# Where VectorE's first instructions of an expert's run stand in its queue: free, or behind the last instructions of the run before

## The chip, the cores and the metric

The kernel runs on one core of one Trainium2 chip. The metric is the device time of one execution in microseconds (us). Five engines work side by side, each through a queue of its own, in order: TensorE (PE in the profile; PEld are its weight loads), VectorE (DVE), ScalarE (ACT), GpSimd (POOL) and SyncE (SP), which issues most of the DMAs.

## The reference

Two blocks follow each other. A gated linear recurrence makes 3072 tokens of 384 numbers; then a router picks one of eight experts for each token, and the token goes through that expert's two layers.

```python
for t in range(S):
    state = alpha[:, :, t, :, None] * state + einsum(k[:, :, t], v[:, :, t])
    y[:, :, t] = einsum(q[:, :, t], state)
...
logits = xn @ en.T / tau                 # xn, en: rows of length 1
expert_idx = argmax(logits, axis=1)
gate_w = softmax(logits) at expert_idx
for e in range(E):
    h = maximum(x[mask] @ w1[e], 0.0)    # 384 -> 1024
    out[mask] = gate_w[mask, None] * (h @ w2[e])
```

## The kernel before, in words

The first part (to about 160 us) is the recurrence, in 24 chunks of 128 tokens. Each token's row, with its logits, is written to a scratch area in DRAM, sorted by expert. The second part takes the experts one after another: run `i` is the `i`-th expert in turn, `run(i)` at L1255. Run 0 has one block of 128 tokens left (two were done early), each of the runs 1 to 7 has three blocks, and behind each run a conditional part (`run_extra`, L1319) does half a block of 64 more tokens if the expert has that many. The branch of that part reads the count on every engine (L1322, L1326).

What a run of three blocks (`pair` in the code) does:

- `first_layer_blocks` (L1080): the first layer in 20 products of sums of quarters, in place of 24 plain ones. A product (L1095) is two matmuls in the code and four in the trace. The products go through four PSUM banks, called A, G, D and B. `put` (L1103, ScalarE) copies a bank into the hidden tile `hT`; `add` (L1109, VectorE) adds a bank to it. A bank is used again and again within the run, so the next product into D can start only when the `add` that reads D is done.
- `mix_hidden` (L1016, VectorE) makes sums of hidden quarters in `hT_m`; `mix_weights` (L1005) makes four sums of quarters of `w2` in `w_m`. `mix_weights` is on GpSimd, except in run 1, where it is on VectorE (L1266). `second_layer` (L967) does one block plainly, and `second_layer_pair` (L1179) two blocks with these sums; its three `gated` steps (L1202) on VectorE read the banks and make the output rows `y`, which `scatter` (L860, GpSimd) sends out by indirect DMA.
- For the next expert: `prepare` (L940) turns its tokens over on TensorE; `begin_gates` (L944) is the first part of its gates, five small VectorE instructions on 128x4 or 128x32 elements (`gtop`, `xg` times `used`, `none`, `sx`, `gsh`) that need only that its rows `xg` have arrived from DRAM; `gates_norm` and `gates_end` are the rest. `mix_first_weights` (L1041, GpSimd) makes 16 sums of quarters of `w1`, `mix_first_rows` (L1054, VectorE) 13 sums of the tokens, for the products of the next run.

Run 0 is not of that kind: it goes through `first_layer` (L957), `prepare_gates(1)` (L950), `mix_first_rows(1)` and one `second_layer`, whose scaling by the gate (L976) is on VectorE.

What sets the order: the program is traced in the order of the text. A planner at compile time then lays out each engine's queue. An instruction whose inputs are there can be placed ahead of earlier ones that still wait, also ahead of the branch of a conditional part, which is placed as one unit. `tc.issue_after(x)` puts what is traced under it behind `x` in `x`'s queue; it orders the queue and waits for nothing. The kernel uses this for chains by hand. `by_dve` (L988) puts every call behind the one before it and keeps the latest in the list `dve`; `by_act` (L993) does so on ScalarE with `act`, `product` on TensorE with `pe`. In a pair run everything that VectorE does up to `gates_end` is in that chain, in this order: in run 1 the four `mix_weights` first, then `begin_gates(i + 1)`, then the 14 `add`s. At the head of a run the list is set anew:

```python
dve[:] = [] if pair else ready
```

An empty list means that the first call of the chain has no place to keep. So a run's first VectorE calls may be placed far ahead, in the middle of the run before.

Of the kernel before, what the change touches and what calls it, by code (L numbers as in the profile page):

```python
# [27 lines left out]
def kernel(  # L28
# [12 lines left out]
    nc = tc.nc  # L41
# [113 lines left out]
    def blocks_run(i):  # L155

        return NC - EARLY if i == 0 else NC

    def slots(i):
        return [(t, P) for t in range(blocks_run(i))] + [(blocks_run(i), HALF)]  # L160
# [40 lines left out]
    with ExitStack() as c1:  # L201
# [517 lines left out]
        for s in range(NS + 3):  # L719
# [64 lines left out]
            if 4 <= s < 4 + NXG * (NC + 1):  # L784
                i, t = divmod(s - 4, NC + 1)
# [41 lines left out]
    with ExitStack() as c3:  # L827
# [66 lines left out]
        def gates(xg, gate, col, n, has=None):  # L894
            known = gates_logits(xg, col, n, has)
            for t in range(n):
                gates_square(xg, known, t)
            gates_norm(known, n)
            return gates_end(gate, known, n)
# [21 lines left out]
        def gates_square(xg, known, t, by=freely):  # L921
            x2 = yp.tile([P, DM], FP32, name="gx2", bufs=1)
            by(nc.scalar.activation, x2, xg[:, t, 0:DM], AF.Square, accum_out=known[1][:, t])

        def gates_norm(known, n, by=freely, by_act=freely):
            sh, sq = known
            shp = [P, n, E]
            by_act(nc.scalar.activation, sq, sq, AF.Sqrt)
            by(nc.vector.tensor_scalar, sq, sq, 1e-6, None, ALU.add)
            by(nc.vector.reciprocal, sq, sq)  # L930
            by(nc.vector.tensor_tensor, sh, sh, sq.to_broadcast(shp), ALU.mult)
            by_act(nc.scalar.activation, sh, sh, AF.Exp)

        def gates_end(gate, known, n, by=freely):
            sh, _ = known
            by(nc.vector.tensor_reduce, gate.unsqueeze(2), sh, axis=AX.X, op=ALU.add)
            by(nc.vector.tensor_scalar, gate, gate, 1e-9, None, ALU.add)
            return by(nc.vector.reciprocal, gate, gate)

        def prepare(i, t, by=None):  # L940
            _, n = slots(i)[t]
            return turn(xg_s[i % NXG][:, t], xT_s[i % 2][:, :, t * P : t * P + n], n, by)

        def begin_gates(i, by):  # L944
            n = len(slots(i))
            return gates_logits(
                xg_s[i % NXG][:, 0:n], sx_s[i % NG][:, 0:n], n, used[:, i, 0:n], by
            )

        def prepare_gates(i):  # L950
            n = len(slots(i))
            return gates(
                xg_s[i % NXG][:, 0:n], gt_s[i % NG][:, 0:n], sx_s[i % NG][:, 0:n], n,
                used[:, i, 0:n],
            )
# [27 lines left out]

        dve = []

        act = []

        def by_dve(call, *args, **kwargs):  # L988
            with turn_of(dve):
                dve[:] = [call(*args, **kwargs)]  # L990
            return dve[0]

        def by_act(call, *args, **kwargs):  # L993
            with turn_of(act):
                act[:] = [call(*args, **kwargs)]  # L995
            return act[0]
# [8 lines left out]
        def mix_weights(w2_t, by):  # L1005

            (b11, b12), (b21, b22) = quarters(w2_t)
            t1, t2, t3, t4 = (w2_m[:, k] for k in range(4))
            for to, x, y in ((t1, b12, b11), (t2, b22, t1), (t3, b22, b12), (t4, b21, t2)):
                by(to, x, y, ALU.subtract)  # L1010
# [5 lines left out]
        def mix_hidden(hT, between):  # L1016

            (a11, a12), (a21, a22) = (hidden(hT, t) for t in range(2))
            s1, s2, s3, s4 = (hT_m[:, k] for k in range(4))
            v = nc.vector  # L1020
            by_dve(v.tensor_tensor, s3, a11, a21, ALU.subtract)
            by_dve(v.tensor_tensor, s1, a21, a22, ALU.add)
            between()
            by_dve(v.tensor_tensor, s2, s1, a11, ALU.subtract)
            by_dve(v.tensor_tensor, s4, a12, s2, ALU.subtract)
# [5 lines left out]
        def rows_x(xT):  # L1031

            return [xT[:, k, t * TH : (t + 1) * TH] for t in range(2) for k in range(KT)]
# [4 lines left out]
        def sum_x(j):  # L1038
            return xT_m[:, j - 6]
# [14 lines left out]
        def mix_first_rows(i):  # L1054

            xT, v = xT_s[i % 2], nc.vector
            x = rows_x(xT) + [sum_x(j) for j in range(6, 19)]

            def minus_sum(to, a, b):
                v.scalar_tensor_tensor(  # L1060
                    out=x[to], in0=x[a], scalar=-1.0, in1=x[b], op0=ALU.mult, op1=ALU.subtract
                )

            for to, a, b, op in (
                (8, 3, 4, ALU.add), (6, 0, 2, ALU.subtract), (7, 1, 6, ALU.add),
                (9, 7, 5, ALU.subtract), (11, 4, 7, ALU.add),
            ):
                v.tensor_tensor(x[to], x[a], x[b], op)
            minus_sum(13, 0, 5)
            for to, a, b, op in (  # L1070
                (12, 0, 4, ALU.subtract), (14, 2, 5, ALU.add), (18, 1, 4, ALU.add),
            ):
                v.tensor_tensor(x[to], x[a], x[b], op)
            minus_sum(17, 8, 9)
            for to, a, b, op in (
                (15, 3, 5, ALU.subtract), (10, 0, 3, ALU.add), (16, 0, 1, ALU.add),
            ):
                v.tensor_tensor(x[to], x[a], x[b], op)

        def first_layer_blocks(w1_t, xT, hT, between, squares):  # L1080

# [173 lines left out]
        def run(i):  # L1255

            w1_t, w2_t = w1_s[i % NW], w2_s[i % NW]
            xT = xT_s[i % 2]
            n = blocks_run(i) * P
            nxt = slots(i + 1) if i + 1 < E else []  # L1260
            hT = hp.tile([P, FT, NC * P], FP32, name="hT", bufs=1)[:, :, 0:n]
            pair = blocks_run(i) == NC
            dve[:] = [] if pair else ready
            if pair:
                if i == 1:
                    mix_weights(w2_t, lambda *args: by_dve(nc.vector.tensor_tensor, *args))  # L1266
                else:
                    mix_weights(w2_t, nc.gpsimd.tensor_tensor)
                left, late = list(range(len(nxt))), list(range(len(nxt)))
                if nxt:  # L1270
                    known = begin_gates(i + 1, by_dve)

                def between():
                    if left:
                        prepare(i + 1, left.pop(0), lambda *args: by_act(nc.scalar.copy, *args))

                def squares():
                    if late:
                        gates_square(xg_s[(i + 1) % NXG], known, late.pop(0), by_act)

                def norm():
                    if nxt:
                        gates_norm(known, len(nxt), by_dve, by_act)

                first_layer_blocks(w1_t, xT, hT, between, squares)
                mix_hidden(hT, norm)
                if nxt:
                    gates_end(gt_s[(i + 1) % NG][:, 0 : len(nxt)], known, len(nxt), by_dve)
            else:
                for f in range(FT):  # L1290
                    done = first_layer(w1_t, hT, xT[:, :, 0:n], f, n)
                    if f % 2 == 1 and f // 2 < len(nxt):
                        turned = prepare(i + 1, f // 2)
            if nxt:
                if pair:
                    mix_first_weights(i + 1, nc.gpsimd.tensor_tensor)
                with turn_of(dve):
                    mix_first_rows(i + 1)
            if nxt and not pair:
                with tc.issue_after(done.ins), tc.issue_after(turned.ins):  # L1300
                    prepare_gates(i + 1)
            if not nxt:

                with turn_of(done_pair):
                    drained.append(nc.gpsimd.drain())
            gate, col = gt_s[i % NG], sx_s[i % NG]
            for t in range(2 if pair else 0, blocks_run(i)):
                sent = second_layer(
                    w2_t, hT[:, :, t * P : (t + 1) * P], gate[:, t : t + 1], col[:, t : t + 1],
                    (lambda *args: by_act(nc.scalar.mul, *args)) if pair  # L1310
                    else nc.vector.tensor_scalar_mul,
                )
            if not pair:

                done_pair.append(sent)
            if pair:
                second_layer_pair(w2_t, hT, gate, col)
# [62 lines left out]
        for t in range(EARLY):  # L1380
            if t == EARLY - 1:
                for b in range(len(slots(0))):
                    prepare(0, b)
                ready = [prepare_gates(0)]
# [44 lines left out]
```

## Time and profile before

| | |
|---|---|
| median of 3 runs | 413.72 us (412.76 to 414.55) |
| profiled execution: its time, its span | 416.3 us, 414.6 us |
| TensorE busy | 398.9 us, 96% of the span |
| VectorE, GpSimd, ScalarE busy | 259.3, 252.7, 205.4 us |
| mean granted TensorE clock | 0.988 |
| first matmul of run 1, end of the last matmul | 188.05 us, 408.96 us |

The profiled execution took 416.3 us, 2.6 us over the median of the plain runs; its span from the first to the last instruction is 414.6 us, so 1.7 us lie outside of the span. Times in the trace are counted from the span's start. A line of the timeline gives the start, the duration, the engine, the line of the code, the operation, output and input with their shapes, how many instructions were merged, and in brackets how long the engine was idle before it and what ended that. A line of the windows gives a stretch of time, then for PE, PEld, DVE, ACT and POOL the busy time and the number of instructions, then the granted TensorE clock, the busy share of the DMA engines and their GB/s.

In the second part the three-block runs follow each other at about 30 us each, or 34 to 35 us with half a block behind them. The first part of the gates stands one run ahead of its own: that of expert 2 (traced in run 1) starts at 189.72 us, within run 0; those of experts 3 to 7 start at 208.85, 239.54, 268.63, 302.27 and 336.83 us, within the runs 1 to 5, each between the 13th and the 14th `add`.

### The profile page before, as it was taken

What the parts mean: (1) busy time and instruction counts of PE and PEld (TensorE: products, weight loads), DVE (VectorE), ACT (ScalarE), POOL (GpSimd) and SP (SyncE); (2) the same over time, 40 slices, a digit from 0 to 9 for tenths busy, and PEclk for the clock granted to TensorE, in tenths of its full rate; (3) what the DMA queues carried; (4) which work ended last, traced back from release to release, by engine and by line L of the source; (5) the groups of instructions that cost most, each with busy time, mean ns of one, the idle gap of its engine ahead of it and who ended that gap; (6) DMA issues with size and microseconds to landing.
All of it is one profiled execution on the core that took longest, in us unless ns stands there. A gap on an engine that the chain in (4) does not pass through costs nothing. (4 is left out here: it accounts for less than half of the span.)

```text
span 414.6 us, 12189 instructions
## 1 busy us (share of the span) xinstructions
PE 398.9 (96%) x4688; PEld 354.6 (86%) x4688; DVE 259.3 (63%) x655; ACT 205.4 (50%) x516; POOL 252.7 (61%) x344
## 2 busy tenths in 40 slices
PE   8999999999999989999999999999999999899994
PEld 8889989888898768588979979989979979879974
DVE  4999979788889514792583572680582375374640
ACT  3455545554455532653673753662672482492520
POOL 6365687677766434771837939937837755946301
PEclk9999999999999996999999999999999999999998
DMA  9999999998986992495802903703800910100101
GB/s 140 155 166 155 155 185 188 195 193 157 191 174 125 344 371 86 136 344 180 290 16 68 344 19 115 291 19 94 315 20 21 337 50 19 40 2 16 40 16 45
DMA packets 119539, 60.26 MB, mean 145 GB/s; under 512 B 102447, under 2 KB 113976, under 8 KB 119472
## 3 DMA queue, kind: packets, MB, share of 16 engines
q1 hardware_dynamic: 115368, 49.15, 50.2%
q0 software_dynamic: 3728, 10.16, 6.9%
q8 instruction: 44, 0.72, 0.7%
q14 instruction: 23, 0.19, 0.2%
q10 hardware_dynamic: 376, 0.05, 0.1%
HBM read 49.69 MB, written 11.45 MB: 147 GB/s over the span
## 5 line engine op out<-in xcount | busy, mean ns | idle before, releaser
L990 DVE TENSOR_TENSOR hT<-hT,pq 128x384 f32<-128x384 f32 x84 | 45.5, 553 | 50.9 <-PE pq L1098 31.3
L860 POOL DMA_INDIRECT out_dram<-y,sx x25 | 24.6, 983 | 65.9 <-ACT y L995 42.4
L513 POOL TENSOR_TENSOR qs<-qc,a 128x512 f32<-128x512 f32 x24 | 30.6, 1276 | 37.0 <-DVE a L509 15.9
L1098 PE MATMUL pq<-xT_m,w_m 128*128 128x192 f32 x252 | 45.4, 326 | 0.0
L973 PE MATMUL pyo<-w,hT 128*128 128x384 f32 x128 | 42.6, 486 | 0.0
L1098 PEld LDWEIGHTS pq<-xT_m,w_m 128*128 128x128 f32 x252 | 40.8, 190 | 0.0
L973 PEld LDWEIGHTS pyo<-w,hT 128*128 128x128 f32 x128 | 24.0, 190 | 14.8
L312 POOL DMA_INDIRECT xs<-x,dest x24 | 24.2, 1009 | 17.8 <-DVE x L656 10.1
L480 DVE TENSOR_TENSOR_SCAN r<-pa,inr 128x511 f32<-128x511 f32 x24 | 29.2, 1216 | 9.0 <-PE pa L195 8.6
L995 ACT ACTIVATE hT<-hT 128x384 f32<-128x384 f32 x56 | 28.4, 518 | 12.2 <-DVE hT L990 9.6
L1010 POOL TENSOR_TENSOR w_m<-w 128x768 f32<-128x768 f32 x12 | 22.6, 1883 | 17.4 <-PE pq L1195 17.4
L1052 POOL TENSOR_TENSOR w_m<-w,w_m 128x256 f32<-128x256 f32 x42 | 30.1, 729 | 3.8 <-PE pq L1098 2.4
L192 PE MATMUL sc<-qs,kr 64*64 64x128 f32 x768 | 29.4, 273 | 2.1 <-issue 2.1
L509 DVE TENSOR_TENSOR_SCAN a<-pa,ini 128x512 f32<-128x512 f32 x24 | 29.3, 1223 | 1.1
L1195 PE MATMUL pq<-w_m,hT_m 128*128 128x192 f32 x168 | 28.5, 327 | 0.2 <-issue 0.2
L1052 POOL TENSOR_TENSOR w_m<-w 128x256 f32<-128x256 f32 x36 | 26.3, 742 | 3.7 <-PE pq L1098 2.4
L1195 PEld LDWEIGHTS pq<-w_m,hT_m 128*128 128x128 f32 x168 | 27.4, 190 | 0.5 <-issue 0.5
L192 PEld LDWEIGHTS sc<-qs,kr 64*64 64x64 f32 x768 | 22.7, 134 | 4.6 <-issue 4.2
L192 PE MATMUL pyx<-sm,vt 128*64 128x128 f32 x384 | 26.3, 279 | 0.0
L652 ACT COPY lg<-pyx 128x32 f32<-128x32 f32 x24 | 4.4, 185 | 40.8 <-PE px L192 34.7
L192 PEld LDWEIGHTS pyx<-sm,vt 128*64 128x64 f32 x384 | 20.5, 136 | 4.1 <-issue 3.6
L624 ACT COPY ycols<-pyx 128x256 f32<-128x256 f32 x48 | 17.9, 377 | 9.4 <-PE pyx L192 5.9
(230 smaller groups left out, 1003.6 us busy)
## 6 DMA issues: line engine op xcount, KB each, us to landing
w<-in_moe_w_dram SPq DMA_DIRECT2D x12, 1536.0 KB
kt<-in_k_dram SPq DMA_DIRECT2D x24, 192.0 KB
qt<-in_q_dram SPq DMA_DIRECT2D x24, 192.0 KB
vt<-in_v_dram SPq DMA_DIRECT2D x24, 192.0 KB
xg<-xs SPq DMA_DIRECT2D x22, 196.5 KB
at<-in_alpha_dram SPq DMA_DIRECT2D x24, 168.0 KB
w<-in_moe_w_dram SPq DMA_DIRECT2D x6, 512.0 KB
w<-in_moe_w_dram SPq DMA_DIRECT2D x8, 384.0 KB
```

What stands on the lines that cost most here:

```text
L192: last["pe"] = nc.tensor.matmul(*args, **kwargs)
L312: ins = nc.gpsimd.indirect_dma_start(out=xs, out_offset=bass.IndirectOffsetOnAxis(ap=rows, axis=0), in_=x, in_offset=None, bounds_check=E ...
L480: nc.vector.tensor_tensor_scan(r[:, L - 2 :: -1], pa[:, L - 1 : 0 : -1], inr[:, L - 2 :: -1], 1.0, ALU.mult, ALU.add,)
L509: d["a_scan"] = by_dve = nc.vector.tensor_tensor_scan(a, pa, ini, 0.0, ALU.mult, ALU.add)
L513: by_pool = nc.gpsimd.tensor_tensor(qs.rearrange("p n t -> p (n t)"), d["qc"], a, ALU.mult)
L860: ins = nc.gpsimd.indirect_dma_start(out=out, out_offset=bass.IndirectOffsetOnAxis(ap=col, axis=0), in_=y, in_offset=None, bounds_check=N - 1,
L973: pe[:] = [nc.tensor.matmul(py, lhsT=hT[:, f], rhs=w2_t[:, f], start=(f == 0), stop=(f == FT - 1),)]
L990: dve[:] = [call(*args, **kwargs)]
L995: act[:] = [call(*args, **kwargs)]
L1052: by(w[to], w[x], w[y], op)
L1098: pe[:] = [nc.tensor.matmul(to[:, f], lhsT=w[left][:, f * P : (f + 1) * P], rhs=x[right], start=start and f == 0, stop=stop, skip_group_ch ...
L1195: pe[:] = [nc.tensor.matmul(to, lhsT=left[:, f], rhs=right[:, f], start=start and f == 0, stop=stop and f == n - 1, skip_group_check=True,)]
```

## The change

At the head of a pair run the chain no longer starts from an empty list but from `before_dve`: the last VectorE instruction of `mix_first_rows` for this run, which was traced in the run before, and, where that was run 0, also the last instruction of `prepare_gates(1)` and the scaling of run 0's output. `mix_first_rows` now returns its last instruction. No arithmetic, tile, DMA or engine changes.

```diff
+        before_dve = []
...
             for to, a, b, op in (
                 (15, 3, 5, ALU.subtract), (10, 0, 3, ALU.add), (16, 0, 1, ALU.add),
             ):
-                v.tensor_tensor(x[to], x[a], x[b], op)
+                ins = v.tensor_tensor(x[to], x[a], x[b], op)
+            return ins
...
-            dve[:] = [] if pair else ready
+            dve[:] = before_dve if pair else ready
...
                 with turn_of(dve):
-                    mix_first_rows(i + 1)
+                    before_dve[:] = [mix_first_rows(i + 1)]
             if nxt and not pair:
                 with tc.issue_after(done.ins), tc.issue_after(turned.ins):
-                    prepare_gates(i + 1)
+                    before_dve.append(prepare_gates(i + 1))
...
                     (lambda *args: by_act(nc.scalar.mul, *args)) if pair
-                    else nc.vector.tensor_scalar_mul,
+                    else lambda *args: before_dve.append(nc.vector.tensor_scalar_mul(*args)),
```

## The prediction

> **What bounds the kernel now.** I read the windows first, then TensorE's waits, then the timelines of the engines around the branch behind run 0. In the second part TensorE is full:
>
> ```profile
> 255.00:289.00 34.00, 33.99 (x290) 30.99 (x289) 17.44 (x46) 17.00 (x39) 25.76 (x26) 1.00 0.42 143
> 289.00:323.00 34.00, 34.00 (x290) 31.34 (x291) 17.21 (x46) 17.72 (x40) 22.45 (x24) 1.00 0.36 127
> ```
>
> PE is busy for 33.99 and 34.00 of 34 us, VectorE (third) for half. A VectorE instruction moved here shows in the time only if TensorE is made to wait, or no longer has to. TensorE's waits from 186 us to the end are all of these:
>
> ```profile
> PE pq L1098 <- PEq L1326: 1.7, 2, 1.3
> PE pyo L1233 <- DVE y L976: 0.3, 1, 0.3
> PE pq L1195 <- issue: 0.2, 1, 0.2
> ```
>
> The 1.7 us are the branch of the conditional part, which the change leaves alone. So little can be won; what can be lost has no such bound.
>
> **What the change takes away.** Two waits for `xg` reach TensorE. In VectorE's timeline:
>
> ```profile
> 189.72 0.19 DVE L990 TENSOR_REDUCE gtop<-xg 128x4 f32<-128x32 f32 x1 [2.51 <-DMA xg<-xs]
> ...
> 190.40 0.61 DVE L976 TENSOR_SCALAR y<-pyo,gt 128x384 f32<-128x384 f32 x1
> ...
> 191.34 0.18 DVE L892 RECIPROCAL gt<-gt 128x4 f32<-128x4 f32 x1
> ...
> 195.48 0.41 DVE L1251 TENSOR_SCALAR y<-pyo,gt 64x192 f32<-64x192 f32 x1 [3.97 <-PE pyo L1246]
> 196.88 1.02 DVE L990 TENSOR_TENSOR hT<-hT,pq 128x384 f32<-128x384 f32 x2 [0.99 <-ACT hT L995]
> ```
>
> Gates 2 stand ahead of run 0's scaling (L976) and wait 2.51 us for their rows; the scaling could start at about 188.3, where its matmuls end, and starts at 190.40. TensorE loses the 0.33 us of L976 above. In run 2 gates 4 wait 1.52 us (at 239.54), and from the run's first transposes to the next run's first matmul TensorE takes 252.60 - 226.19 = 26.41 us, against 351.07 - 325.09 = 25.98 us in run 5: 0.43 us. The wait of 0.89 us in run 3 (at 268.63) costs 26.00 - 25.98, nothing. Run 6 has no gates of a later expert in its middle and takes 381.15 - 355.17 = 25.98 us, just as the runs 4 and 5 that have them: five small instructions fewer in the middle win nothing. Gain: 0.33 + 0.43 = about 0.75 us.
>
> **What it moves: gates 3 to 7.** In runs 1 to 5 they would go behind `mix_first_rows` (ends 218.8 in run 1). The first `gated` step (218.73) is ready and comes first, then VectorE is idle 1.62 us until 220.77: room for five instructions that took 0.19 + 0.16 + 0.17 + 0.16 + 0.18 us at 189.72. But GpSimd's `mix_weights` starts at 219.44 (1.80 us); by the next paragraph `sx` may have to wait for its end at 221.24. The second `gated` step would then run at 221.3 instead of 220.77; TensorE needs it before its product at 221.79, so the slack of 0.6 us is just used up. From both sides: 0 if all pass or are put behind the third `gated` step (3.29 us idle follow it), 1.9 us in each of five runs, 9.5 us, if `gsh` waits for GpSimd's next sum too (until 223.1). I take 0: in the five groups in mid-run two instructions got through between two sums of GpSimd every time.
>
> **What it moves: the first sums of run 1.** The chain's first call in run 1 is not the gates but the four sums of `mix_weights`, which run 1 makes on VectorE. They now stand at 165.05 to 169.83, the first of them:
>
> ```profile
> 165.05 0.95 DVE L990 TENSOR_TENSOR w_m<-w 128x768 f32<-128x768 f32 x1
> ```
>
> Ahead of all of run 0, where they cost nothing (TensorE is busy for 10.00 of the 10 us from 160 to 170), and where leaving gains nothing. With the change they queue behind L976 and the last gate instruction of run 0 (191.34 in the lines above). The next things in VectorE's queue are the branch and L1251 of the half block. Behind the four sums come gates 2 and the 14 `add`s of run 1, so whatever the sums take behind the branch delays the first `add`, now at 196.88.
>
> How many fit ahead of the branch? TensorE's queue has six matmuls of run 1 ahead of it (1.14 us at 188.05), ScalarE's one `put`. So the branch was placed about 1.1 us behind run 0's last matmul. L976 and the three gate steps behind it take 191.52 - 190.40 = 1.12 us of that on VectorE, and only then are the sums free to be placed. Room for none, at most for one. I take none: all four fall behind the branch, and behind L1251, though VectorE idles 3.97 us ahead of it.
>
> **Their cost.** Shifted by the 0.33 us won above, L1251 ends at 195.56. Alone, four sums take 4 x 0.87 = 3.5 us (168.88 to 169.75, start to start), the gates 0.75 us (189.72 to 190.47), so `add` would start at 199.8 and end at 200.35. But GpSimd has 14 sums of `mix_first_weights` to do from 197.56 on, and both read SBUF:
>
> ```profile
> 209.12 0.72 POOL L1052 TENSOR_TENSOR w_m<-w_m 128x256 f32<-128x256 f32 x1
> 209.92 0.74 POOL L1052 TENSOR_TENSOR w_m<-w 128x256 f32<-128x256 f32 x1
> ```
>
> ```profile
> 190.29 0.18 DVE L990 TENSOR_TENSOR gsh<-xg,gtop 128x32 f32<-128x32 f32 x1
> ...
> 209.98 0.73 DVE L990 TENSOR_TENSOR gsh<-xg,gtop 128x32 f32<-128x32 f32 x1
> ```
>
> The same `gsh` takes 0.18 us with GpSimd quiet and 0.73 us beside a sum of GpSimd, and ends with it. That is what the Trainium skill says (SBUF — State Buffer, "Who interferes with whom"): a VectorE instruction with two SBUF inputs and a GpSimd instruction that reads SBUF exclude each other for a whole instruction. An `add`, with one input in PSUM, keeps its 0.55 us throughout. So two sums run until 197.3 us, then the engines alternate: 0.73 + 0.87 twice, to 200.5 us; the gates take some 1.6 us so (1.86 us from 208.85 to 210.71, less part of the `add` between them), to 202.1 us; the first `add` ends at 202.65.
>
> Who waits for it? TensorE's second product into bank D, the bank which this `add` reads:
>
> ```profile
> 197.11 0.49 PE L885 MATMUL pxg<-ident,xg 128*128 128x128 f32 x3
> 197.43 2.77 PE L1098 MATMUL pq<-xT_m,w_m 128*128 128x192 f32 x16
> ```
>
> The 16 matmuls are the second products into A, G, D and B at 0.65 us each; D's starts at 197.43 + 1.30 = 198.73, and the `add` has 1.3 us to spare today. It moves to 202.65: 3.9 us later. All behind it in TensorE's queue moves along, and a full engine wins nothing back. That contains the 0.33 us already. Without the exclusion it would move to 200.35, 1.6 us, and the whole would be 413.7 + 1.6 - 0.43 = 414.9 us; row and rule together decide for the larger figure.
>
> **The clock.** TensorE would stand still for 202.65 - 198.4 = 4.25 us. The skill (TensorE: Matmul & The Clock Gate, "What's actually happening") lets the clock fall to half after one idle window of about 3.4 us and rise after one busy window. The trace is harsher. Windows of 1 us around an idle time of only 1.73 us (152.98 to 154.79):
>
> ```profile
> 153.00:154.00 1.00, 0.06 (x5) 0.00 (x0) 0.00 (x0) 0.00 (x0) 0.48 (x1) 1.00 1.05 376
> 155.00:156.00 1.00, 1.00 (x20) 0.91 (x12) 0.00 (x0) 0.72 (x5) 0.00 (x0) 0.54 0.39 140
> 161.00:162.00 1.00, 1.00 (x7) 0.91 (x5) 0.00 (x0) 0.38 (x1) 0.00 (x0) 0.54 0.54 201
> ```
>
> Half clock for 0.92 + 5 + 0.92 = 6.8 us, two such windows, which cost 3.4 us. By the rule a 4.25 us stall costs 1.7 us (3.4 us at half speed), by the row 3.4 us; if the low clock falls inside the stall, less, down to 0. I take 1.7 us.
>
> **The sum,** made on the profiled execution (416.3 us, of which the span is 414.6): +3.9 - 0.43 + 1.7 = +5.2 us. The profiled execution is 2.6 us over the median of plain runs; the difference is carried over: 413.7 + 5.2 = 418.9 us.
>
> **Rivals.**
>
> All or most sums fit ahead of the branch. From 189.3 us (L976 no longer waits) to 195.5 us VectorE has 6 us for 3.5 us of sums and 0.75 us of gates, GpSimd is quiet, and only the gain is left: 413.7 - 0.75 = 413.0 us. For it speaks that GpSimd's queue has all four of its `mix_weights` ahead of the later branches; against it, that those were ready 4 us earlier. With two ahead of the branch, the other two end at 197.35, gates at 198.9, `add` at 199.45: 0.7 us late, 414.0 us. This is where it turns: at two or more sums ahead of the branch the change costs nothing to speak of.
>
> One sum ahead of it: the rest end at 197.3 + 0.73 + 0.87 = 198.9, the gates at 200.5, the first `add` at 201.05, so 2.3 us late; less 0.43, plus 0 to 1.7 for the clock: 415.6 to 417.3 us.
>
> The gates of the later runs block the second `gated` step: up to 9.5 us; alone, with the sums of run 1 at no cost, 413.0 + 9.5 = 422.5 us.
>
> That the change orders nothing is excluded: the sums and the gates stand ahead of `mix_first_rows` now (165.05 against 181.20; 208.85 against 215.26).
>
> **How the numbers follow.** No sum ahead of the branch 0.45 (417.2 to 420.6, by the clock; predicted 418.9); one 0.28 (415.6 to 417.3); two or more 0.21 (413.0 to 414.0); a loss in the later runs that decides 0.06 (over 415.8). About 0.5%, or 2.1 us, is what a measurement of this kernel can tell from no change. Slower: 0.45 + 0.23 of the 0.28 + 0.06 = 0.74. Same: 0.05 + 0.19 = 0.24. Faster by over 2.1 us: 0.02, since TensorE's waits leave no room. The range goes from the gain alone, 413.0, to the highest of the likeliest case, 420.6.
>
> **What would show it.** The four sums of `w_m` on VectorE start at about 195.6 us, the later two next to GpSimd's sums; TensorE has one wait of about 4 us for VectorE's `hT` near 198.4 us, then a dip of the granted clock. The wait of L1233 for L976 is gone, `gtop` waits for no DMA, and run 2 takes 26.0 us between the same two points. Gates 3 to 7 stand among the `gated` steps. I am wrong if the sums stand before 192 us, if `add` doesn't move, or if TensorE stalls in runs 2 to 6.

## The result, and the profile after

| | before | after |
|---|---|---|
| median of 5 plain runs each | 414.37 us (412.76 to 414.55) | 420.06 us (418.1 to 421.85) |
| profiled execution: time, span | 416.3, 414.6 us | 418.1, 416.4 us |
| mean granted TensorE clock in it | 0.988 | 0.988 |
| VectorE busy | 259.3 us | 269.9 us |

The ratio of the times is 1.0129, with an interval from 1.0083 to 1.0175: 5.4 us slower, 3.4 to 7.3. The forecast was 418.9 us. The profiled execution of the changed kernel is the fastest of its five, 2.0 us under their median, so its trace shows less of the loss than the runs have. Up to the first matmul of run 1 it is even 0.98 us ahead of the trace of before (187.07 and 188.05 us), 0.95 of it gained ahead of 161 us, where nothing was moved.

The queues of TensorE, ScalarE, GpSimd and SyncE are the same as before, instruction by instruction; only VectorE's order differs. The new lines shift the line numbers by two or three: `by_dve` is L992, the products of the first layer L1101, those of the second layer L1198, the gated steps L1205, the half block's scaling L1254, the branch L1329, and run 0's scaling, now a lambda, L1314.

The windows of the changed kernel, with the same columns as before:

```profile
196.00:198.00 2.00, 1.35 (x9) 1.05 (x7) 2.00 (x2) 1.46 (x3) 1.94 (x4) 1.00 1.01 398
198.00:200.00 2.00, 0.10 (x1) 0.10 (x1) 1.93 (x8) 0.00 (x0) 0.85 (x1) 1.00 1.07 389
...
256.00:290.00 34.00, 33.97 (x289) 31.00 (x288) 19.19 (x46) 16.73 (x38) 25.02 (x26) 1.00 0.42 143
```

Away from run 1 TensorE is as full as it was. From 197.35 to 199.90 us it stands, and VectorE is the engine that is full. TensorE's waits from 186 us to the end are now these:

```profile
PE pq L1101 <- DVE hT L992: 2.5, 1, 2.5
PE pq L1101 <- PEq L1329: 1.8, 1, 1.8
```

The wait of the half block for run 0's scaling (0.3 us) has gone, as forecast; one of 2.5 us for `hT` has come. What VectorE does in that time stands in its timeline:

```profile
188.31 0.93 DVE L992 TENSOR_TENSOR w_m<-w 128x768 f32<-128x768 f32 x1
193.94 0.41 DVE L1254 TENSOR_SCALAR y<-pyo,gt 64x192 f32<-64x192 f32 x1 [4.70 <-PE pyo L1249]
194.27 0.94 DVE L992 TENSOR_TENSOR w_m<-w,w_m 128x768 f32<-128x768 f32 x1
195.13 0.94 DVE L992 TENSOR_TENSOR w_m<-w 128x768 f32<-128x768 f32 x1
196.00 2.27 DVE L992 TENSOR_TENSOR w_m<-w,w_m 128x768 f32<-128x768 f32 x1
...
198.29 0.58 DVE L992 TENSOR_TENSOR xg<-xg,used 128x4 f32<-128x4 f32 x1
...
199.29 1.01 DVE L992 TENSOR_TENSOR hT<-hT,pq 128x384 f32<-128x384 f32 x2
```

One sum got ahead of the branch. VectorE then idled 4.70 us in front of the half block's scaling (L1254), and the other three sums came behind it, with gates 2 behind them. The last sum took 2.27 us in place of 0.94. GpSimd's timeline has three sums of `mix_first_weights` beside it, two of which end before VectorE's sum gets through:

```profile
196.02 1.43 POOL L1054 TENSOR_TENSOR w_m<-w 128x256 f32<-128x256 f32 x2
197.50 1.36 POOL L1054 TENSOR_TENSOR w_m<-w,w_m 128x256 f32<-128x256 f32 x1
```

The first of two merged `add`s, 199.29 to about 199.84, is what TensorE's product waits for:

```profile
195.88 1.47 PE L1101 MATMUL pq<-xT_m,w_m 128*128 128x192 f32 x8
199.90 1.57 PE L1101 MATMUL pq<-xT_m,w_m 128*128 128x192 f32 x8 [2.55 <-DVE hT L992]
```

By stages, from the first matmul of a run to that of the next, in us:

| | run 1 | run 2 | run 3 | run 4 | run 5 | run 6 |
|---|---|---|---|---|---|---|
| before | 35.04 | 29.51 | 29.32 | 34.59 | 34.56 | 30.08 |
| after | 37.35 | 29.13 | 29.10 | 34.77 | 34.75 | 30.64 |

Run 1 loses 2.3 us, run 2 wins 0.4, the runs 4 and 5 lose 0.2 each. Run 6 has the branch wait in both (1.8 us after, 1.3 before); in other executions this wait turns up behind other runs or behind none, so its 0.5 us says nothing.

The loss of the runs 4 and 5 has its place at the gated steps. VectorE's timeline at the end of run 1, where the gates of expert 3 now stand:

```profile
219.95 0.41 DVE L1205 SCALAR_TENSOR_TENSOR y<-pq,gt,u 128x192 f32<-128x192 f32 x1
...
220.75 1.78 DVE L992 SCALAR_TENSOR_TENSOR sx<-xg,none 128x4 int32<-128x4 f32 x1
...
222.56 0.41 DVE L1205 SCALAR_TENSOR_TENSOR y<-pq,gt,u 128x192 f32<-128x192 f32 x1
```

and GpSimd's:

```profile
220.71 1.81 POOL L1012 TENSOR_TENSOR w_m<-w 128x768 f32<-128x768 f32 x1 [3.35 <-PE pq L1198]
```

`sx`, on 128x4 numbers, took 0.16 us at 199.11 and takes 1.78 us here: GpSimd's sum had begun 0.04 us before it, and both end at 222.5.

### The profile page after: what moved, and what is told of

Read it like the earlier page. It is cut to its first block, busy times and chain, and to the rows that moved or that the text cites. A ratio compares the mean times of both kernels' runs of the same rounds, so it can differ in the third digit from the quotient of the medians.

```text
span 416.4 us, 12190 instructions
## 1 busy us (share of the span) xinstructions
PE 397.8 (96%) x4688; PEld 353.2 (85%) x4688; DVE 269.9 (65%) x655; ACT 205.7 (49%) x516; POOL 249.4 (60%) x344
## 5 line engine op out<-in xcount | busy, mean ns | idle before, releaser
L992 DVE TENSOR_TENSOR hT<-hT,pq 128x384 f32<-128x384 f32 x84 | 45.5, 553 | 50.0 <-PE pq L1101 32.3
L1101 PE MATMUL pq<-xT_m,w_m 128*128 128x192 f32 x252 | 45.7, 327 | 2.5 <-DVE hT L992 2.5
L1101 PEld LDWEIGHTS pq<-xT_m,w_m 128*128 128x128 f32 x252 | 40.8, 190 | 2.8 <-DVE hT L992 2.8
L1012 POOL TENSOR_TENSOR w_m<-w 128x768 f32<-128x768 f32 x12 | 21.7, 1806 | 20.1 <-PE pq L1198 20.1
L1198 PE MATMUL pq<-w_m,hT_m 128*128 128x192 f32 x168 | 28.4, 326 | 0.0
L1198 PEld LDWEIGHTS pq<-w_m,hT_m 128*128 128x128 f32 x168 | 27.5, 190 | 0.0
```

The costliest lines, as they stand in the source:

```text
L1101: pe[:] = [nc.tensor.matmul(to[:, f], lhsT=w[left][:, f * P : (f + 1) * P], rhs=x[right], start=start and f == 0, stop=stop, skip_group_ch ...
L1198: pe[:] = [nc.tensor.matmul(to, lhsT=left[:, f], rhs=right[:, f], start=start and f == 0, stop=stop and f == n - 1, skip_group_check=True,)]
```

## The experiments

Twelve kernels in three batches, each batch on a chip of its own. The kernel before ran beside them each time, with medians of 414.3, 404.4 and 403.9 us; so ratios are compared, not times. The line numbers in these kernels are those of the kernel before. Two theories stood against each other at first. A: the loss is TensorE's wait behind the moved sums, and what follows from that wait. B: the gates of the later runs, which cost a little five times. A third, C, a loss ahead of 160 us, finds nothing in the traces: there the profile after is ahead of the one before.

**The change again.** No edit.

> The changed kernel once more, only to see how far its own times spread and in which stage they do. Theory A (the loss is the stall of TensorE in run 1 behind the sums of w2, with or without a dip of the granted clock after it): 416 to 417 us in executions without a dip, 418 to 421 with one, so the spread of 418.1 to 421.85 shows as low clock between 200 and 210 us. Theory B (the five later runs lose, by gates that block the gated steps for GpSimd's sums): the runs 1 to 5 take more than 26.2 us each from first transposes to the next run's first matmul. Theory C (something ahead of 160 us, where no instruction was moved, differs between executions): the start of the second part moves by over 1 us.

Measured: 420.63 us, ratio 1.014 (1.0091 to 1.019). The wait in run 1 is the same 2.55 us, but in this execution matmuls behind it are slow:

```profile
201.28 2.52 PE L1098 MATMUL pq<-xT_m,w_m 128*128 128x192 f32 x8 [2.55 <-DVE hT L990]
203.59 0.85 PE L885 MATMUL pxg<-ident,xg 128*128 128x128 f32 x3
```

2.52 us in place of 1.57, and 0.85 in place of 0.49. The windows of 1 us (the granted clock is the third number from the end) say why:

```profile
201.00:202.00 1.00, 0.72 (x4) 0.72 (x5) 0.69 (x2) 0.00 (x0) 0.00 (x0) 0.87 1.06 380
202.00:203.00 1.00, 1.00 (x5) 1.00 (x5) 0.00 (x0) 0.45 (x1) 0.34 (x1) 0.50 1.08 379
...
204.00:205.00 1.00, 1.00 (x6) 1.00 (x5) 0.55 (x1) 0.48 (x1) 0.88 (x2) 0.50 0.55 170
205.00:206.00 1.00, 1.00 (x8) 1.00 (x7) 0.00 (x0) 0.46 (x2) 0.42 (x1) 0.93 0.03 5
```

Half clock for 0.26 + 3 + 0.14 = 3.4 us, so 1.7 us lost, and run 1 takes 39.00 us in place of 37.35. The same wait, with and without the dip, in two executions of one order.

A second thing was new. In run 0 VectorE stood without a visible reason, and TensorE then waited 1.4 us for the copy:

```profile
170.96 0.41 DVE L1052 TENSOR_TENSOR w_m<-w 128x256 f32<-128x256 f32 x1
174.53 0.36 DVE L887 COPY xT<-pxg 128x192 f32<-128x192 f32 x1 [3.15 <-remote]
```

The matmuls that this copy reads had ended at 171.2. In the profile after, the same two instructions stand 0.34 us apart. Where the four sums left a hole at 165 us, the planner had put the first sums of `mix_first_weights` (L1052) ahead of run 0's copies; that was a third suspect.

**The sums free, all gates ordered.** In run 1 only:

```diff
-  mix_weights(w2_t, lambda *args: by_dve(nc.vector.tensor_tensor, *args))
+  dve[:] = []; mix_weights(w2_t, lambda *args: by_dve(nc.vector.tensor_tensor, *args)); dve.extend(before_dve)
```

> As the changed kernel, but the four sums of w2 in run 1 keep no place behind run 0; only the gates are ordered. Theory A: no stall in run 1, 413.3 to 414.0 us, no slower than before, ratio 0.997 to 1.001. Theory B: the later runs still lose, ratio about 1.01. Theory C: ratio about 1.01, with no wait of TensorE in run 1.

Measured: 416.41 us, ratio 1.0043 (1.0015 to 1.0071). TensorE has no wait in run 1, VectorE no stand in run 0. Two thirds of the loss are gone, not all.

**The sums ordered, all gates free.**

```diff
-  dve[:] = before_dve if pair else ready
+  dve[:] = (before_dve if i == 1 else []) if pair else ready
-  known = begin_gates(i + 1, by_dve)
+  held, dve[:] = dve[:], []; known = begin_gates(i + 1, by_dve); dve.extend(held)
```

> The other half alone: the four sums of w2 in run 1 are ordered behind run 0, all gates stay free as before. Theory A: the whole loss stays, TensorE waits 2 to 3 us for VectorE's hT in run 1, ratio 1.006 to 1.015. Theory B: ratio 1.000 to 1.003, the loss is gone with the gates.

Measured: 417.72 us, ratio 1.0077 (1.0049 to 1.0106). The wait in run 1 is 1.4 us, since no gates stand between the sums and the `add`. In run 0 of the profiled execution VectorE stands longer still:

```profile
173.51 0.62 DVE L976 TENSOR_SCALAR y<-pyo,egt 128x384 f32<-128x384 f32 x1 [7.33 <-PE pyo L973]
```

TensorE waited 2.2 and 2.1 us for copies behind it. So this ratio mixes two things.

**The sums of run 1 on GpSimd,** the rest as in the change.

```diff
-  if i == 1:
+  if i < 0:
```

> As the changed kernel, but run 1's four sums of w2 are made on GpSimd, as in the later runs (4 x 1.8 us there); the chain of run 1 then begins with the gates. Theory A: no stall in run 1, 413.3 to 414.5 us, ratio 0.997 to 1.003; if it is slower, then because the sums hold up GpSimd's writes of blank rows and with them the rows of a later expert. Theory B: ratio about 1.01.

Measured: 418.55 us, ratio 1.0096 (1.0068 to 1.0125). The wait in run 1 is gone, and another has come in run 0, because GpSimd now makes its sums there. VectorE's timeline:

```profile
169.81 3.81 DVE L892 TENSOR_TENSOR xg<-xg,used 128x2 f32<-128x2 f32 x1
...
174.21 2.50 DVE L892 TENSOR_TENSOR gsh<-xg,gtop 128x16 f32<-128x16 f32 x1
```

GpSimd's timeline beside them:

```profile
168.23 3.60 POOL L1010 TENSOR_TENSOR w_m<-w 128x768 f32<-128x768 f32 x2
171.77 1.82 POOL L1010 TENSOR_TENSOR w_m<-w,w_m 128x768 f32<-128x768 f32 x1
...
174.84 1.82 POOL L1010 TENSOR_TENSOR w_m<-w,w_m 128x768 f32<-128x768 f32 x1
```

Instructions of 0.15 and 0.17 us end with sums of GpSimd that take 1.82 us (`gsh` starts 0.63 us before its sum; what held it until then is not shown). TensorE waited 2.5 and 1.4 us for what stood behind them. Behind the longer of these waits its clock fell to half, for 0.52 + 2 + 0.90 = 3.4 us from 183.5 us on:

```profile
182.94 0.55 PE L885 MATMUL pxg<-ident,xg 128*128 128x128 f32 x3 [2.54 <-DVE xT L887]
```

```profile
183.00:184.00 1.00, 1.00 (x7) 1.00 (x8) 0.97 (x4) 0.00 (x0) 0.70 (x2) 0.74 1.07 385
184.00:185.00 1.00, 1.00 (x7) 1.00 (x6) 0.97 (x4) 0.28 (x1) 0.70 (x2) 0.50 1.03 386
...
186.00:187.00 1.00, 1.00 (x5) 0.76 (x4) 1.00 (x1) 0.97 (x4) 1.00 (x2) 0.55 0.46 174
```

The run moves the loss and so doesn't tell the theories apart; it shows the same hold in a third place.

**Gates 2 alone.** The chain of run 1 starts empty, and `before_dve` is put behind the four sums:

```diff
-  dve[:] = before_dve if pair else ready
+  dve[:] = [] if pair else ready
-  mix_weights(w2_t, lambda *args: by_dve(nc.vector.tensor_tensor, *args))
+  mix_weights(w2_t, lambda *args: by_dve(nc.vector.tensor_tensor, *args)); dve.extend(before_dve)
```

> Only the gates of expert 2 (run 1) are put behind run 0's sums; the four sums of mix_weights keep their early place at 165 us, the gates of experts 3 to 7 their place among the adds. If the whole loss comes from the sums and from the gates of experts 3 to 7, nothing of it is left, and TensorE's 0.3 us wait ahead of run 1 goes: 413.6 to 414.4 us, ratio 0.998 to 1.000. If the loss of the kernel with free sums (+1.8 us) came from gates 2, which the branch splits there, it stays: about 416 us, ratio 1.004. If the planner's new place lets TensorE start earlier with no price: up to 0.75 us faster.

Measured: 403.92 us beside 404.4, ratio 0.9984 (0.9965 to 1.0003). All that TensorE waits for from 140 us on is this:

```profile
PE pq L1195 <- issue: 0.3, 1, 0.3
```

So the order that the change is named for costs nothing and may win a little; it isn't where the loss comes from.

**Gates 3 to 7 alone.**

```diff
-  dve[:] = before_dve if pair else ready
+  dve[:] = (before_dve if i > 1 else []) if pair else ready
```

> Only the gates of experts 3 to 7 (runs 2 to 6) are ordered, which puts them between the first and the second gated step; run 1 is as in the kernel before. By the traces so far a run with the gates there is 0.13 to 0.17 us longer, five times: +0.7 us, 415.0 us, ratio 1.0017. If these gates carry the whole loss of the kernel with free sums: +1.8 us, 416.2 us, ratio 1.004. If they are free, as the prediction took them: 414.3 us, ratio 1.000.

Measured: 405.06 us beside 404.4, ratio 1.0019 (0.9997 to 1.0042). The profile has what the ratio can't settle: the runs 4 and 5 take 34.46 us, and 34.33 us in the kernel with gates 2 alone. See the last experiment for the place.

**The change, and no sum of `mix_first_weights` ahead of run 0's copies.**

```diff
-  prepare(0, b)
+  dve.append(prepare(0, b))
...
-  with turn_of([known]):
+  with turn_of([known] + dve):
       mix_first_weights(1, nc.vector.tensor_tensor)
```

> The change, and the sums of mix_first_weights for run 1 on VectorE are kept behind run 0's two copies of the turned rows, so that none of them stands ahead of these copies or of the first scaling (L976). If a sum that moved ahead is what VectorE stood behind for 3 to 7 us in run 0 (TensorE then waited 1.4 to 4.3 us for the copies), that wait goes and with it 1.4 to 3 us: 417.5 to 419 us, ratio 1.008 to 1.011. If the stand comes from something else in that stretch (a transfer, the row fetches), it stays, and the kernel keeps 420.5 us, ratio 1.014. The 2.5 us wait in run 1 stays either way.

Measured: 409.18 us beside 404.4, ratio 1.0139 (1.0096 to 1.0182): no better than the change. TensorE's wait in run 1 is 2.56 us, with the clock at 1.00 behind it; VectorE doesn't stand in run 0. The third suspect wins nothing back.

**The change, and GpSimd quiet beside the three sums.** In run 1 GpSimd's 16 sums go behind a one-column copy on GpSimd, which reads what the first `add` has written:

```diff
   by_dve(nc.vector.tensor_tensor, c[j], c[j], p, op)
+  probe or probe.append(nc.gpsimd.tensor_copy(yp.tile([P, 1], FP32, name='pr', bufs=1), c[j][:, 0, 0:1]))
...
-  mix_first_weights(i + 1, nc.gpsimd.tensor_tensor)
+  with turn_of(probe if i == 1 else []): mix_first_weights(i + 1, nc.gpsimd.tensor_tensor)
```

> The change, and in run 1 GpSimd's 16 sums of mix_first_weights start only behind the first add (a one-column copy on GpSimd reads that add's output), so that GpSimd does no sums beside VectorE's last three sums and gates 2. If GpSimd's sum held up VectorE's (2.27 in place of 0.94 us, and xg 0.58 in place of 0.15 us), VectorE is 1.7 us earlier and TensorE waits 0.8 us in place of 2.5: 418.5 us, ratio 1.010, and less chance of a lowered clock behind it. If the hold was no cause and the sums' own time is all, the wait stays 2.5 us and the kernel 420.5 us. GpSimd's own sums come 3 us later; if run 2's first products wait for them, it shows at 225 us.

Measured: 406.01 us beside 404.4, ratio 1.0031 (1.001 to 1.0053). VectorE's order is that of the change. Its last sum, its `xg` and its first `add`s, in the timeline:

```profile
186.08 0.94 DVE L990 TENSOR_TENSOR w_m<-w,w_m 128x768 f32<-128x768 f32 x1
...
187.05 0.15 DVE L990 TENSOR_TENSOR xg<-xg,used 128x4 f32<-128x4 f32 x1
...
187.62 1.01 DVE L990 TENSOR_TENSOR hT<-hT,pq 128x384 f32<-128x384 f32 x2
```

TensorE's product behind them, and GpSimd's sums, which now come after the `add`:

```profile
188.22 1.57 PE L1098 MATMUL pq<-xT_m,w_m 128*128 128x192 f32 x8 [0.80 <-DVE hT L990]
```

```profile
188.38 2.78 POOL L1052 TENSOR_TENSOR w_m<-w 128x256 f32<-128x256 f32 x4
```

0.94 and 0.15 us where the change has 2.27 and 0.58: that is 1.76 us, and TensorE's wait is 1.76 us shorter. This run decides between the first two theories. It leaves every gate where the change puts it, takes only GpSimd's work away from beside VectorE's sums, and most of the loss goes. The Trainium skill (SBUF — State Buffer, "Who interferes with whom") has VectorE instructions with two SBUF inputs and GpSimd instructions that read SBUF exclude each other for a whole instruction; the three runs in which GpSimd was moved to or from such a place agree with it.

**The change a third time,** beside the last three.

> The change unaltered, once more, to stand beside the next three on one chip. Ratio 1.013 to 1.014 as twice before, whatever the time of the kernel before is there. By the theory of the lowered clock: of the loss about 2.5 us is the wait in run 1, 0.7 us the gates of experts 3 to 7, and the rest a mean granted clock that is 0.003 to 0.004 lower than in the kernel before. If the clock has no part, the runs of this kernel have the same clock as those of the kernel before.

Measured: 409.46 us beside 403.87, ratio 1.0117 (1.0072 to 1.0161). The wait is 2.56 us again, the clock 1.00 behind it. The median of the mean granted clock is 0.996 in its runs and 0.997 in those of the kernel before; in the batch before, it was 0.994 for the change with run 0's copies ahead, and 0.997 for the kernel before. A dip elsewhere counts in this mean too: the 0.994 of the profiled execution here comes from 3.4 us at half clock from 135.0 us on, behind a wait of 2.01 us for a DMA.

**The sums free, a second time.**

> The kernel with free sums (all gates ordered, the four sums at their early place), once more. Its two halves alone gave 0.9984 and 1.0019, which makes 1.0003; it had given 1.0043 (1.0015 to 1.0071) on another chip. If the halves add up: 0.999 to 1.002. If gates 2 and gates 3 to 7 together cost something that neither costs alone: 1.004 again.

Measured: 404.47 us beside 403.87, ratio 1.0016 (1.0 to 1.0032). That meets the interval of the first time and is near the 1.0003 that the two halves make. The 1.0043 on the first chip need not have a cause of its own.

**The sums ordered, gates free, GpSimd quiet beside them.** The edits of the third and the eighth kernel together.

> Only the four sums are ordered, all gates are free, and GpSimd's 16 sums of run 1 start behind the first add. VectorE's last three sums then take 0.94 us each and no gates stand between them and the first add, so TensorE should wait 0.2 us or not at all in run 1 (0.80 us with the gates there, 1.4 us with the sums alone and GpSimd free). If the reordering of run 0's VectorE queue (sums of mix_first_weights ahead of the copies) costs nothing by itself: ratio 0.999 to 1.002. If it costs the 1.4 to 4.3 us that some traces showed: 1.004 to 1.010.

Measured: 404.38 us beside 403.87, ratio 1.0006 (0.9982 to 1.0031). VectorE's queue in run 0 is that of the third kernel, and here VectorE stands for 1.4 us at most from 155 us to the start of run 1, with an engine to wait for each time. In run 1 the last sum takes 0.95 us, the `add`s follow at once, and no product of the first layer waits:

```profile
188.27 0.95 DVE L990 TENSOR_TENSOR w_m<-w,w_m 128x768 f32<-128x768 f32 x1
189.14 1.00 DVE L990 TENSOR_TENSOR hT<-hT,pq 128x384 f32<-128x384 f32 x2
```

So the move of the sums costs nothing by itself, and neither does the place that the other sums took in run 0.

**Gates 3 to 7 behind the third gated step.** The kernel with gates 3 to 7 alone, and:

```diff
-  gated(y0[:, m:DM], d, g0, u[:, 1])
+  before_dve.append(gated(y0[:, m:DM], d, g0, u[:, 1]))
```

> Only the gates of experts 3 to 7 are ordered, and behind the third gated step of the run before in place of between the first and the second. If their 0.13 to 0.17 us a run comes from the second gated step, which stands behind them and lets TensorE's last product into bank A start: the loss goes, 1.000 (0.8 us below the other place). If it comes from the gates leaving the adds or from their 1.8 us hold by GpSimd wherever they stand: 1.002 as at the other place. If they are in the way of the next run's first adds behind the branch: 1.002 to 1.005.

Measured: 403.88 us beside 403.87, ratio 0.9995 (0.9977 to 1.0014). Between the first and the second gated step (the kernel with gates 3 to 7 alone), on VectorE:

```profile
237.94 1.78 DVE L990 SCALAR_TENSOR_TENSOR sx<-xg,none 128x4 int32<-128x4 f32 x1
...
239.74 0.41 DVE L1202 SCALAR_TENSOR_TENSOR y<-pq,gt,u 128x192 f32<-128x192 f32 x1
```

and the product behind it on TensorE:

```profile
240.29 1.54 PE L1195 MATMUL pq<-w_m,hT 128*128 128x192 f32 x8
```

Behind the third step, on TensorE:

```profile
240.35 1.46 PE L1195 MATMUL pq<-w_m,hT 128*128 128x192 f32 x8
```

The second step ends at 240.15, and the last product needs the bank that it reads. In the one kernel the product starts 1.36 us behind the start of the one before it (238.93) and takes 1.54, in the other 1.30 us (239.05) and 1.46: 0.14 us. The runs 4 and 5 take 34.33 us again. The hold by GpSimd is there in the last kernel too (`none`, of 0.17 us, takes 1.73 us beside a sum of 1.80 us), with no one behind it.

No kernel here beats the one before by more than the measurement can tell; gates 2 alone comes nearest.

## Why the prediction was right, and where its steps were off

The figure was 1.2 us under the median and inside its range. The mechanism held: run 1's sums left their early place and came right ahead of its first `add`, GpSimd's sums held them up, and TensorE waited for that `add`. That the figure fits so well is in part luck. The case that came true is the rival with one sum ahead of the branch, and for it the prediction had 415.6 to 417.3 us, below all five runs. Errors went against each other: the wait was taken 1.7 us too long, gates 3 to 7 were taken at nothing and cost 0.7 us, and where it had 1.7 us for the clock, 2 to 3 us remain whose cause is open.

- **"Gain: 0.33 + 0.43 = about 0.75 us."** The mechanism holds: `gtop` no longer waits ahead of run 0's scaling, the 0.3 us wait of the half block is gone, and run 2 is 0.38 us shorter. Gates 2 alone, which can win only the 0.33, gave 0.6 us, between 1.4 us faster and 0.1 us slower.
- **"I take none: all four fall behind the branch."** Wrong by one: one sum went ahead of it, at 188.31 us, which by its own sign ("before 192 us") speaks against the likeliest case. The rival with one sum had the first `add` 2.3 us late, and run 1 became 2.3 us longer; TensorE's wait is 2.55 us where the likeliest case had 4.25.
- **The exclusion.** Right in kind and place, a little too large: the prediction had 2.3 us for it (3.9 less 1.6), and of the wait's 2.55 us, 1.76 go when GpSimd is quiet. The sums didn't alternate one by one as I had it: VectorE's last sum stood behind two sums of GpSimd (196.02 to 197.45) and ran then.
- **"Ahead of all of run 0, where they cost nothing … and where leaving gains nothing."** Right: the sums ordered with GpSimd quiet gave 1.0006. What I didn't see is that other sums would fill the hole they left; it did no harm that is measured.
- **Gates 3 to 7: "I take 0".** Wrong, though within the bounds of 0 to 9.5 us. `sx` waited for GpSimd's first sum, five times, and got ahead of its second; the slack of 0.6 us ran out by 0.14 us a run. By the traces that is 0.7 us in five runs, and it goes when they stand behind the third step; the ratio of 1.0019 (0.8 us) has an interval that takes in 1.
- **The clock: 1.7 us.** One of four profiled executions with this wait has the dip behind it, and there it costs just 1.7 us: 3.4 us at half clock, the figure of the Trainium skill (TensorE: Matmul & The Clock Gate, "What's actually happening"), not the row's 6.8. It came after 2.55 us, though, less than the idle window of about 3.4 us that the page asks for. The three others have none behind the wait. Each of them is 2.0 to 2.2 us faster than the median of its kernel, the one with it 1.6 us slower, as if most plain runs had it. The mean clocks bear this out in part only. One dip lowers the mean by about 0.004 (an estimate: half of 3.4 us in 405). With run 0's copies ahead, the profiled execution has 0.999 and the plain runs 0.990 to 0.994. But in the change's third run the medians are 0.996 and 0.997, and among the five runs of the result the slowest (421.85 us) has the highest clock, 0.999, and the fastest the lowest, 0.988.

The sum, as measured on the two later chips: the wait 2.6, the gates 0.8, gates 2 less 0.6, makes 2.8 us (neither of the last two is clear of zero), and the loss there is 4.7 to 5.6 us (2.9 to 7.4 with the intervals). What is left, 2 to 3 us, goes with the wait: with GpSimd quiet, 0.8 + 0.8 - 0.6 = 1.0 us is left to explain 1.25 (1.0031 of 404.4 us), and the loss falls by 3.5 to 4.4 us for a wait that is 1.76 us shorter.

The remainder is not in a trace without a dip: with run 0's copies ahead the profiled execution took 3.0 us more than that of gates 2 alone on the same chip (406.98 and 403.98 us), and 2.9 of that is in run 1. It lies in plain runs, of which only time and mean clock are kept. The clock may account for 0.4 to 1.2 us of it by the means (0.001 and 0.003 of about 405 us), for 1.7 if every plain run has the dip; that is argued, not shown. The wait at the branch (0 to 3.7 us) and VectorE's stand in run 0 (1.4 and 4.3 us of TensorE's time) vary between executions as well, and no run here shows whether they are more frequent with the change. So the cause of the remainder is open.

Still open is why VectorE stood in run 0 for 3.15 and 7.33 us in two profiled executions on the first chip. The first had the order of the profile after, of the change's third run and of the change with GpSimd quiet, the second that of the sums ordered with GpSimd quiet; none of these shows such a stand. Order alone isn't the cause.

## What to carry to other kernels

A chain that is given a new start moves its first link, whatever that is: look up what is called first, here four sums of 0.94 us ahead of the gates that were meant. Work that is free in one place is paid in another, first where two engines hold each other up, as VectorE and GpSimd do here: ask for each moved VectorE instruction what GpSimd does beside it, and how much slack stands between its end and the next matmul. And a wait of TensorE can cost more than its own length, here 2.55 us and then 1.7 us of lowered clock in one execution.

## What the runs showed of the hardware

- A VectorE instruction on a few numbers can be held for one sum of GpSimd or for several in a row: `sx` takes 0.16 us alone and 1.78 us beside a sum of 1.81 us, `xg` 0.15 us alone and 3.81 us with the sums on GpSimd: it starts 0.26 us before the end of one sum and is held through the next two, to 173.59 us.
- The granted clock fell to half for 3.4 us behind a wait of 2.55 us in one execution and not in three others with the same wait (2.55, 2.56 and 2.56 us). It also fell for 3.4 us behind waits of 2.54 us (the sums on GpSimd) and 2.01 us (the change a third time), and not behind 2.23 and 2.14 us (the sums ordered, gates free). In the trace of before it fell for 6.8 us after 1.73 us. So the length of a wait alone doesn't tell in these traces.
- TensorE's wait at the branch (L1326) is 0 to 3.7 us in all, in kernels with the same instructions on TensorE, and behind different runs. A difference of 2 us between two profiled executions can be just that.
